# Second experts taken group by group, three token pairs each, with seven-block second products

## The chip, the core and the metric

The kernel runs on one core of a Trainium2 chip, as one launch. TensorE multiplies (PE in the profile) and writes into PSUM; VectorE (DVE), ScalarE (ACT) and GpSimd (POOL) work on what lies in SBUF and, the first two, in PSUM; SyncE (SP) issues nearly all transfers. The metric is the device time of one execution in microseconds; the median of several executions is compared.

## The reference

An attention without softmax, a dense expert with SiLU, and a mixture of four experts with ReLU, whose outputs are weighted with normed probabilities:

```python
def _attn_ref(q, k, v, g_norm) -> np.ndarray:
    kv = np.einsum('bhsd,bhse->bhde', k, v)
    out = np.einsum('bhsd,bhde->bhse', q, kv)
    rms = np.sqrt(np.mean(out * out, axis=-1, keepdims=True) + 1e-06)
    return (out / rms * g_norm).astype(np.float32)
...
    h = x @ w_in
    g = h * (1.0 / (1.0 + np.exp(-h)))
    return (g @ w_out).astype(np.float32)
...
    N, D = x.shape
    E = w1.shape[0]
    p = domain_probs / (domain_probs.sum(-1, keepdims=True) + 1e-09)
    out = np.zeros((N, D), dtype=np.float32)
    for e in range(E):
        h = np.maximum(x @ w1[e], 0.0)
        out += p[:, e:e + 1] * (h @ w2[e])
    return out.astype(np.float32)
```

There are 2304 tokens with 512 features. The dense expert has 2048 hidden features, each of the four others 1024. All is float32.

## The kernel before

**Tiling.** Tokens are cut into three stretches of 768, which the code and this text call pairs, since each holds two halves of 384 columns. Hidden features are cut into groups of 512: four of the dense expert ("first experts", `E1 = 4`), eight of the others ("second experts", `E2 = 8`, two for each expert). A step `n` is one group with one pair. Steps -12 to -1 are the first experts, steps 0 to 23 the second. A step has a first product (features to 512 hidden features) and a second one (hidden back to 512 features, summed into `acc`).

**Precision.** A float32 operand is split into an upper half, which ScalarE writes (`hi`), and a lower half, the rest, which VectorE or GpSimd writes (`lo`). A product of two operands takes three matmuls of halves, 12 matmuls of 128x128 by 128x384 for each of its quarters.

**Seven products.** The operands of a step are two-by-two blocks. By Strassen's scheme in Winograd's form seven products of block sums stand for eight: 84 matmuls for a whole product. A first product is always made so (`first`, blocks into banks `x` and `z` of PSUM). A second product is made so in some steps (`again`: banks `ox`, `oz`; it needs seven hidden operands, c11, c12 taken as t1, t2, t3, t4, c22 and c21, so four differences by `sumh`, and seven additions into `acc` by `gather`), and in the others as four plain blocks of 24 matmuls, 96 in all (`second`: bank `o`; four hidden operands, four gathers). `seven(n)` says which: before, `n >= 8` and five of the first experts' steps.

**Order.** `events` gives each call a time in slots; the calls are sorted by it, and each engine gets its instructions in that order. A slot is one block of 12 matmuls: in a step's window the first products stand at odd slots (`b0 + 1 + 2k`) and the second products of the step before at even ones (`after + 2m`, where `after` is the next step's start). A step with seven second products lasts 14 slots, one with plain ones 15. Each engine runs its queue in order, so an instruction that waits holds up what is queued behind it.

**Loops before.** The second experts run pair by pair: step `n` is pair `n // 8` with group `n % 8`. The features' operands of a pair (`x`, seven tiles of 768 KB, split by `xhi` and `xlo`) stay in SBUF for its eight steps. In the first eight steps the weights are loaded, summed (`sumw`), split (`op1`, `op2`) and put away to DRAM (`put_away`, 14 tiles of 512 KB to a group); steps 8 to 23 get them from there (`get`), eight slots ahead of use. The weight sums of the second products, for which there is no use in plain steps, are made beside steps 0 to 7 too. Pairs 0 and 1 leave after their last step, while the next pair runs: `leave` turns 256 tokens by eight transposes, ScalarE copies them, and ScalarE's queue issues the store. `leave_last` does it for the last pair at the end.

## Time and profile before

| | before |
|---|---|
| median of 3 runs | 1168.19 us (1168.1 to 1168.59) |
| the profiled execution | 1168.03 us, its span 1166.2 us |
| TensorE busy | 1153.6 us, 99% |
| VectorE busy | 866.8 us, 74% |
| ScalarE busy | 499.1 us, 43% |
| GpSimd busy | 315.5 us, 27% |
| granted TensorE clock, mean | 1.0 |
| moved by DMA | 309 MB, 265 GB/s in the mean |

Busy times say which engine is nearly full; the chain that ended last says whose work set the end; a timeline shows where an engine stood still and for whom. Matmuls overlap, so the mean duration of one (335 ns) is not what one costs: that is the distance from start to start. In the windows below, the first number behind a stretch is its length, and then come the busy us of each engine with its count of instructions.

### The profile page before, as it was taken

What the parts mean: (1) busy time and instruction counts of PE and PEld (TensorE: products, weight loads), DVE (VectorE), ACT (ScalarE), POOL (GpSimd) and SP (SyncE); (2) the same over time, 40 slices, a digit from 0 to 9 for tenths busy, and PEclk for the clock granted to TensorE, in tenths of its full rate; (3) what the DMA queues carried; (4) which work ended last, traced back from release to release, by engine and by line L of the source; (5) the groups of instructions that cost most, each with busy time, mean ns of one, the idle gap of its engine ahead of it and who ended that gap; (6) DMA issues with size and microseconds to landing.
All of it is one profiled execution on the core that took longest, in us unless ns stands there. A gap on an engine that the chain in (4) does not pass through costs nothing.

```text
span 1166.2 us, 17617 instructions
## 1 busy us (share of the span) xinstructions
PE 1153.6 (99%) x6769; PEld 1144.8 (98%) x6769; DVE 866.8 (74%) x1010; ACT 499.1 (43%) x720; POOL 315.5 (27%) x196
## 2 busy tenths in 40 slices
PE   9999999999999999999999999999999999999998
PEld 8999999999999999999999999999999999999997
DVE  3997566887887667777777866777888866666776
ACT  4895565455544445434344324333233333233222
POOL 4943311232221324222232312121114221111112
PEclk9999999999999999999999999999999999999999
DMA  9876877566556366987896869898988777878764
GB/s 369 345 270 228 331 256 261 200 212 245 198 189 227 137 203 227 325 296 279 303 324 260 287 222 360 319 330 312 332 312 285 244 258 255 275 258 283 252 199 126
DMA packets 101815, 309.00 MB, mean 265 GB/s; under 512 B 11420, under 2 KB 37988, under 8 KB 101220
## 3 DMA queue, kind: packets, MB, share of 16 engines
q1 hardware_dynamic: 99716, 304.69, 73.6%
q10 hardware_dynamic: 2016, 3.18, 0.7%
q8 instruction: 54, 0.88, 0.3%
q14 instruction: 29, 0.24, 0.1%
...
## 4 chain that ended last, share of the span: by engine, by line
PE 54%; DVE 6%; ACT 2%; issue 2%; DMA 0%; SPq 0%; DVEq 0%; ACTq 0%
PE ps_x L390 15%; PE ps_z L390 11%; PE ps_o L526 10%; PE ps_ox L390 10%; PE ps_oz L390 8%; DVE f L469 1%; ACT hid L164 1%; DVE acc L495 1%; DVE f L433 1%; DVE hid L167 1%; DVE t L477 1%; DVE w L167 1%; PE ps_t L556 0%; DVE s L308 0%; ACT x L164 0%
## 5 line engine op out<-in xcount | busy, mean ns | idle before, releaser
L390 PE MATMUL ps_x<-x,w 128*128 128x384 f32 x1584 | 297.0, 335 | 0.0
L390 PEld LDWEIGHTS ps_x<-x,w 128*128 128x128 f32 x1584 | 277.6, 188 | 0.0
L526 PE MATMUL ps_o<-hid,w 128*128 128x384 f32 x1440 | 268.3, 335 | 1.5 <-ACT hid L164 1.4
L526 PEld LDWEIGHTS ps_o<-hid,w 128*128 128x128 f32 x1440 | 251.2, 188 | 3.4 <-ACT hid L164 2.4
L164 ACT ACTIVATE hid<-f 128x768 fp32r<-128x768 f32 x143 | 120.1, 843 | 243.3 <-DVE f L469 217.5
L390 PE MATMUL ps_z<-x,w 128*128 128x384 f32 x1188 | 222.9, 335 | 0.6 <-DVE f L433 0.6
L390 PEld LDWEIGHTS ps_z<-x,w 128*128 128x128 f32 x1188 | 208.2, 188 | 0.9 <-DVE f L433 0.9
L390 PE MATMUL ps_ox<-hid,w 128*128 128x384 f32 x1008 | 190.2, 336 | 1.2 <-DVE acc L495 1.0
L390 PEld LDWEIGHTS ps_ox<-hid,w 128*128 128x128 f32 x1008 | 176.2, 188 | 2.1 <-ACT hid L164 0.9
L167 DVE TENSOR_TENSOR hid<-f,hid 128x768 fp32r<-128x768 f32 x116 | 124.3, 1072 | 60.6 <-ACT hid L164 59.4
L390 PE MATMUL ps_oz<-hid,w 128*128 128x384 f32 x756 | 142.1, 335 | 1.6 <-DVE acc L495 1.2
L390 PEld LDWEIGHTS ps_oz<-hid,w 128*128 128x128 f32 x756 | 131.9, 188 | 2.7 <-DVE acc L495 2.1
L167 POOL TENSOR_TENSOR hid<-t,hid 128x768 fp32r<-128x768 f32 x32 | 62.7, 1961 | 241.8 <-ACT hid L164 236.0
L167 POOL TENSOR_TENSOR hid<-f,hid 128x768 fp32r<-128x768 f32 x27 | 52.3, 1938 | 210.7 <-ACT hid L164 210.7
L167 POOL TENSOR_TENSOR w<-raw,w 128x512 fp32r<-128x512 f32 x41 | 60.9, 1491 | 178.3 <-ACT w L164 135.2
L164 ACT ACTIVATE hid<-t 128x768 fp32r<-128x768 f32 x64 | 53.9, 843 | 121.0 <-DVE t L477 121.0
L495 DVE TENSOR_TENSOR acc<-ps_ox,acc 128x768 f32<-128x768 f32 x77 | 73.2, 950 | 41.7 <-PE ps_ox L390 41.6
L222 POOL TENSOR_TENSOR full<-full,wd_raw 128x512 int32<-128x512 int32 x32 | 47.7, 1491 | 127.7 <-DVE full L216 93.1
L433 DVE TENSOR_TENSOR f<-ps_z,f 128x768 f32<-128x768 f32 x66 | 62.6, 949 | 20.2 <-PE ps_z L390 20.2
L164 ACT ACTIVATE w<-s 128x512 fp32r<-128x512 f32 x88 | 54.3, 623 | 49.6 <-DVE s L249 18.1
L469 DVE SCALAR_TENSOR_TENSOR f<-f,pb 128x768 f32<-128x768 f32 x72 | 72.5, 1006 | 3.3 <-DMA pb<-p_dram 1.2
L495 DVE TENSOR_TENSOR acc<-ps_oz,acc 128x768 f32<-128x768 f32 x61 | 58.1, 952 | 20.1 <-PE ps_oz L390 19.2
...
## 6 DMA issues: line engine op xcount, KB each, us to landing
...
x<-x_dram SPq DMA_DIRECT2D x63, 768.0 KB, 4.6
raw<-in_w SPq DMA_DIRECT2D x192, 128.0 KB, 3.8
...
x_dram<-x SPq DMA_DIRECT2D x21, 768.0 KB, 6.0
...
```

The costliest lines, as they stand in the source:

```text
L164: self.nc.scalar.activation(t[:, 0], f, AF.Copy)
L167: (eng or self.nc.vector).tensor_tensor(t[:, 1], f, t[:, 0].bitcast(F32), op=ALU.subtract)
L222: self.nc.gpsimd.tensor_tensor(f, f, self.words(c, i, 0, I32), op=ALU.add)
L390: self.nc.tensor.matmul(p[:, f, :HN], w[0][:, a, c : c + 128], x[:, b, kp, :], start=self.FRESH[k] and a == b == kp == 0, stop=b == kp == ...
L433: self.nc.vector.tensor_tensor(t, self.of_ps(n, c), t, op=ALU.add)
L469: self.nc.vector.scalar_tensor_tensor(f, src, 0.0, self.probs(n, int(name[2]) - 1), op0=ALU.max, op1=ALU.mult)
L477: self.nc.vector.tensor_tensor(f, self.f[n, a], self.f[n, b], op=ALU.subtract)
L495: self.nc.vector.tensor_tensor(a, self.of_ps(n, k), a, op=ALU.add)
L526: self.nc.tensor.matmul(self.ps[n, b][:, e, :HN], w[:, u, c : c + 128], h[:, v, kp, :], start=self.count[key] == 1, stop=self.count[key] = ...
```

## The change

The second experts run group by group: step `n` is group `n // 3` with pair `n % 3`, as the first experts did. A group's weights are loaded, summed and split once, in the steps around its first (`weight_events`, with the slots of `W1_AT` and `W2_AT`), and stay in SBUF for three steps. Nothing of them goes to DRAM. The features' operands do: steps 0 to 2 split them (`X_AT`), use them and put them into DRAM, and every later step gets its seven tiles from there (`xget`, 12.4 slots ahead of use). All steps but step 0 have seven second products; step 0 keeps the plain blocks. The differences of hidden parts are written into tiles that are no longer needed, in place of five tiles of their own. The lower halves of t3, t4 and c22 go to GpSimd in all steps from 1 on. All three pairs end in the last three steps, so all six pieces of pairs 0 and 1 leave at the end: one just before the last step's second products, five between them, from SyncE's queue.

```diff
-            self.start[n + 1] = self.start[n] + (self.LONG if n <= E2 else self.SHORT)
+            self.start[n + 1] = self.start[n] + 7 + (7 if self.seven(n - 1) else 8)
...
-        return n >= E2 or n in (-8, -7, -5, -4, -3)
+        return n >= 1 or n in (-8, -7, -5, -4, -3)
...
+    def whi(self, e, i, name):
+        pool, tag = (self.w1_p, "w1") if i == 1 else (self.v_p, "w2b") if name in ("s3", "s4") else (self.w2_p, "w2")
+        t = pool.tile([128, 2, 512], F32R, tag=tag, name=f"w{i}")
+        self.halves[e, i, name] = t, self.raw[e, i, name]
+        self.hi(*self.halves[e, i, name])
+        if i == 1:
+            self.wf[e, self.A.index(name)] = t
+        else:
+            self.w2["f", e, name] = t
...
-    def put_away(self, n, i, k):
-        t = self.w1[n, k] if i == 1 else self.w2[n, self.A[k]]
-        self.nc.sync.dma_start(out=self.w_dram[n * 14 + (i - 1) * 7 + k], in_=t.bitcast(F32).rearrange("p a b -> p (a b)"))
...
+    def slot(self, n, k):
+
+        return 5 - k if k in (2, 3) and (n < 0 or n == 1) else k
...
-        w = self.wf[self.group(n), k] if n < 0 else self.w1.pop((n, k))
-        self.product(self.ps[n, self.INTO[k]], (w, 1), self.x[self.key(n), self.B[k]], k)
-        if n < 0:
+        w = self.wf[self.group(n), k]
+        self.product(self.ps[n, self.INTO[k]], (w, 1), self.x[n, self.B[k]], k)
+        if 0 <= n < NP:
+            self.done_x(n, self.B[k])
+        else:
             del self.x[n, self.B[k]]
-            if self.pair(n) == NP - 1:
-                del self.wf[self.group(n), k]
+        if self.pair(n) == NP - 1:
+            del self.wf[self.group(n), k]
...
-            self.ps[n, b] = self.bank(self.ps2, b, "o")
+            self.ps[n, b] = self.bank(self.ps2, b + (n > -3), "o")
...
-    def leave(self, n, t, b):
-        p = self.bank(self.ps2, n + 1, "t")
+    def leave(self, t, b, pool, i):
+        p = self.bank(pool, i, "t")
         for k in range(2):
             for d in range(KC):
                 c = (b + k) * 128
                 self.nc.tensor.transpose(p[:, k, d * 128 : d * 128 + 128], self.acc[:, t, d, c : c + 128], self.ident)
-        for k in range(2):
-            o = self.o_p.tile([128, DM], F32, tag="o2", name="o2")
-            self.nc.scalar.activation(o, p[:, k, :], AF.Copy)
-            r = t * PW + (b + k) * 128
-            self.nc.scalar.dma_start(out=self.out[r : r + 128, :], in_=o)
+        o = self.x_p.tile([128, 2, DM], F32, tag=f"x{t * 3 + b // 2}", name="o2")
+        self.nc.scalar.activation(o, p, AF.Copy)
+        r = t * PW + b * 128
+        self.nc.sync.dma_start(out=self.out[r : r + 256, :].rearrange("(k p) c -> p k c", p=128), in_=o)
...
+        on_pool = {name: self.nc.gpsimd for name in (("t3", "t4") if n < 0 else ("c22", "t3", "t4"))}
+        late = 0 <= n < self.steps - 1
+        c11, c21, t4 = (5.8, 4.7, 5.6) if late else (4.7, 3.3, 4.6)
+        for at, name in ((b0 + c11, "c11"), (b0 + 10.7, "c22"), (b0 + 12.4, "t1"), (after + 1.11, "t2"), (after + 2.4, "t3"),
+                         (after + c21, "c21"), (after + t4 + 0.9, "t4")):
...
-            lo = at + (0.5 if at < b0 + 12 else 0.005)
-            put(lo, self.hlo, n, name, pool if name in ("t3", "t4") else None, True)
+            lo = at + (0.5 if at < b0 + 12 or late and name == "c21" else 0.005)
+            put(lo, self.hlo, n, name, on_pool.get(name), True)
...
+    X_AT = (
+        ((-12.5, -10.5, -6.7, -8.7, -4.7, -2.7, -0.7), (-11.5, -7.5, -6.5, -1.6)),
+        ((-12.8, -11, -6.8, -8.7, 4.6, 3, 8.2), (-13.8, -7.3, 3.9, 7.3)),
...
+    W1_AT = dict(
+        load=(-23.2, -13), s1=(-11, -7.6), s2=(-10.9, -7.5), s4=(-4.9, -5.1), s3=(-6.9, -4.5),
...
+        b0, i = self.start[(e - E1) * NP], min(e - E1, 1)
+        for at, part in ((self.W1_AT, 1), (self.W2_AT, 2)):
+            load = self.load1 if part == 1 else self.load2
+            for k, (r, c) in enumerate(((1, 0), (1, 1), (0, 0), (0, 1))):
+                put(b0 + at["load"][i] + 0.5 * k, load, e, r, c)
+            for name in ("s1", "s2", "s3", "s4"):
+                put(b0 + at[name][i], self.sumw, e, part, name)
+        ops = dict(zip(self.A, self.W1_AT["op"][i])), self.W2_AT["op"][i]
+        on_pool = (self.A if i == 0 else ("a12", "s3", "a22")), (("a11", "a21", "a22") if i == 0 else ())
+        for part in (1, 2):
+            for name, at in ops[part - 1].items():
+                put(b0 + at, self.whi, e, part, name)
+                put(b0 + at + 0.4, self.flo, e, part, name, pool if name in on_pool[part - 1] else None)
...
+                    put(b0 + at[k], self.xhi, n, name)
+                    put(b0 + at[k] + 0.01, self.xlo, n, name, pool if k in ((0, 1, 5) if n else (1, 3, 5)) else None)
+                    put(b0 + at[k] + 2.5, self.xput, n, name)
+                for k, s in enumerate(sums):
+                    put(b0 + s, self.xsum, t, f"t{k + 1}")
+            else:
+                for k in range(7):
+                    put(self.start[n - 1] + 2 * k + 2.6, self.xget, n, k)
...
-                put(i - lead, self.op1, n, k, pool if k in (1, 4, 6) or n == 0 else None)
-                put(i - lead + 2, self.put_away, n, 1, k)
...
-                for m, k in enumerate(self.ORDER):
-                    put(after + 2 * m, self.again, n, k)
-                    put(after + 2 * m - self.LEAD, self.get, n, 2, k)
...
-            elif q == E2 - 1:
-                for k in range(PW // 256):
-                    put(self.start[n + 3 + k] + 11.5, self.leave, n + 2 + k, t, 2 * k)
...
+                for slot, name in ((5.3 if n else 6.15, "c11"), (10.5, "c22"), (12.5, "c12"), (14.1, "c21")):
+                    put(b0 + slot, self.hhi, n, name)
+                    put(b0 + slot + 0.01, self.hlo, n, name, pool if name == "c22" else None)
+                self.plain_events(put, n)
+        end = self.start[self.steps]
+        for k, at in enumerate((-2.5, 1.3, 2.8, 4.3, 5.8, 7.3)):
+            where = (self.ps2, self.steps + 1) if at < 0 else (self.ps1, k + 1)
+            put(end + at, self.leave, k // 3, k % 3 * 2, *where)
+        for b, (slot, j, i, *ds) in enumerate(((9.5, 1, 0), (11.5, 1, 1), (13, 0, 0), (16, 0, 1, (0,)), (16, 0, 1, (1,)))):
+            put(end + slot, self.leave_last, j, i, b, *ds)
```

On TensorE, the second product of step 1 among the first product of step 2 (`ps_x`, `ps_z`). Before, it is plain blocks into `ps_o`:

```order
L390 MATMUL ps_x<-x_3748,w_4447 128x384 x12
L526 MATMUL ps_o<-hid,w_4431 128x384 x6
L526 MATMUL ps_o<-hid,w_4452 128x384 x6
L390 MATMUL ps_z<-x_3788,w_4485 128x384 x12
L526 MATMUL ps_o<-hid,w_4431 128x384 x6
L526 MATMUL ps_o<-hid,w_4452 128x384 x6
```

After:

```order
L366 MATMUL ps_ox<-hid,w_4115 128x384 x12
L366 MATMUL ps_x<-x_4287,w_3719 128x384 x12
L366 MATMUL ps_oz<-hid,w_4097 128x384 x12
L366 MATMUL ps_z<-x_4323,w_3753 128x384 x12
L366 MATMUL ps_ox<-hid,w_4496 128x384 x12
L366 MATMUL ps_x<-x_4401,w_3794 128x384 x12
```

The two halves of a plain block, each of two weights by six matmuls, have become seven blocks of one weight by twelve, into two banks by turns.

On VectorE, in the middle of a seven-product step. Before, in a step of the last two thirds (`t` are the differences' tiles, `acc` the gathers, `f<-f,pb` the products with the probabilities):

```order
L167 TENSOR_TENSOR hid<-f,hid 128x768
L433 TENSOR_TENSOR f<-ps_z,f 128x768
L469 SCALAR_TENSOR_TENSOR f<-f,pb 128x768
L495 TENSOR_TENSOR acc<-ps_ox,acc 128x2x384
L167 TENSOR_TENSOR hid<-f,hid 128x768
L495 TENSOR_TENSOR acc<-ps_oz,acc 128x2x384
L495 TENSOR_TENSOR acc<-ps_ox,acc 128x2x384
L433 TENSOR_TENSOR f<-ps_x,f 128x768
```

After, the same place in the first step of a group (`s` are weight sums, `raw` loaded weights, `w` split ones):

```order
L149 TENSOR_TENSOR hid<-f,hid 128x768
L149 TENSOR_TENSOR w_5679<-s,w_5679 128x512
L149 TENSOR_TENSOR w_5699<-raw_5518,w_5699 128x512
L464 TENSOR_TENSOR acc<-ps_oz,acc 128x2x384
L289 TENSOR_TENSOR s<-raw_5494,raw_5511 128x512
L289 TENSOR_TENSOR s<-s,raw_5518 128x512
L149 TENSOR_TENSOR w_5727<-s,w_5727 128x512
L149 TENSOR_TENSOR w_5744<-s,w_5744 128x512
L464 TENSOR_TENSOR acc<-ps_ox,acc 128x2x384
L289 TENSOR_TENSOR s<-raw_5535,s 128x512
L289 TENSOR_TENSOR s<-raw_5518,raw_5494 128x512
L411 TENSOR_TENSOR f<-ps_x,f 128x768
```

Between a step's gathers now stand four weight sums and four lower halves of weights.

On TensorE at the end, the transposes `ps_t` of the pieces that leave. Before:

```order
L390 MATMUL ps_ox<-hid,w_10594 128x384 x12
L390 MATMUL ps_oz<-hid,w_10623 128x384 x12
L390 MATMUL ps_ox<-hid,w_10652 128x384 x12
L390 MATMUL ps_oz<-hid,w_10684 128x384 x12
L390 MATMUL ps_ox<-hid,w_10722 128x384 x12
L569 MATMUL ps_t<-ident,acc 128x128 x6
L390 MATMUL ps_oz<-hid,w_10747 128x384 x12
```

After:

```order
L366 MATMUL ps_ox<-hid,w_9619 128x384 x12
L522 MATMUL ps_t<-ident,acc 128x128 x8
L366 MATMUL ps_oz<-hid,w_9647 128x384 x12
L522 MATMUL ps_t<-ident,acc 128x128 x8
L366 MATMUL ps_ox<-hid,w_9664 128x384 x12
L522 MATMUL ps_t<-ident,acc 128x128 x16
L366 MATMUL ps_oz<-hid,w_9788 128x384 x12
L522 MATMUL ps_t<-ident,acc 128x128 x8
L366 MATMUL ps_ox<-hid,w_9855 128x384 x12
L534 MATMUL ps_t<-ident,acc 128x128 x6
```

Five pieces of eight transposes have come between the last second products; the smaller pieces of the last pair (by six) follow as before.

## Rows read from the trace of the kernel before

**Rows 1.** Page, part 1: busy us, share of the span, instructions

```profile
PE 1153.6 (99%) x6769; PEld 1144.8 (98%) x6769; DVE 866.8 (74%) x1010; ACT 499.1 (43%) x720; POOL 315.5 (27%) x196
```

**Rows 2.** Chain that ended last: start us, us, work

```profile
600.57 4.17 PE ps_o L526 x24
```

**Rows 3.** Waits of TensorE: waiter, releaser, us in total, times, longest

```profile
PE ps_o L526 <- ACT hid L164: 1.4, 3, 0.6
PE ps_oz L390 <- DVE acc L495: 1.2, 2, 1.0
```

**Rows 4.** Timeline of TensorE around two stalls: start, us, instruction, [idle before]

```profile
568.13 2.25 PE L526 MATMUL ps_o<-hid,w 128*128 128x384 f32 x12
...
573.28 2.25 PE L390 MATMUL ps_x<-x,w 128*128 128x384 f32 x12
...
917.22 2.25 PE L390 MATMUL ps_oz<-hid,w 128*128 128x384 f32 x12
920.07 2.36 PE L390 MATMUL ps_z<-x,w 128*128 128x384 f32 x12 [0.60 <-DVE f L433]
...
924.99 1.21 PE L390 MATMUL ps_x<-x,w 128*128 128x384 f32 x6
```

**Rows 5.** Groups by form: instruction, count, busy us, mean ns, idle before

```profile
L167 DVE TENSOR_TENSOR hid<-f,hid 128x768 fp32r<-128x768 f32 x116 | 124.3, 1072 | 60.6 <-ACT hid L164 59.4
...
L495 DVE TENSOR_TENSOR acc<-ps_ox,acc 128x768 f32<-128x768 f32 x77 | 73.2, 950 | 41.7 <-PE ps_ox L390 41.6
L469 DVE SCALAR_TENSOR_TENSOR f<-f,pb 128x768 f32<-128x768 f32 x72 | 72.5, 1006 | 3.3 <-DMA pb<-p_dram 1.2
...
L167 POOL TENSOR_TENSOR hid<-f,hid 128x768 fp32r<-128x768 f32 x27 | 52.3, 1938 | 210.7 <-ACT hid L164 210.7
...
L308 DVE TENSOR_TENSOR s<-raw,raw 128x512 f32<-128x512 f32 x32 | 32.0, 1000 | 0.0
...
L477 DVE TENSOR_TENSOR f<-f 128x768 f32<-128x768 f32 x20 | 22.0, 1098 | 1.9 <-ACT f L443 1.8
...
L167 DVE TENSOR_TENSOR w<-raw,w 128x512 fp32r<-128x512 f32 x15 | 12.2, 821 | 11.8 <-ACT w L164 9.4 <-DMA raw<-in_w 2.4
```

**Rows 6.** Timeline of VectorE beside GpSimd in the first experts

```profile
231.58 1.54 POOL L167 TENSOR_TENSOR w<-s,w 128x512 fp32r<-128x512 f32 x1 [13.90 <-ACT w L164]
231.89 2.05 DVE L477 TENSOR_TENSOR f<-f 128x768 f32<-128x768 f32 x1
...
241.23 1.74 POOL L167 TENSOR_TENSOR w<-full,w 128x512 fp32r<-128x512 f32 x1
241.74 0.94 DVE L495 TENSOR_TENSOR acc<-ps_oz,acc 128x768 f32<-128x768 f32 x1
242.61 1.17 DVE L167 TENSOR_TENSOR hid<-f,hid 128x768 fp32r<-128x768 f32 x1
```

**Rows 7.** Busy us of each engine in stretches of 50 us

```profile
250.00:300.00 50.00, 48.61 (x278) 48.00 (x277) 39.65 (x55) 24.62 (x36) 9.92 (x8) 1.00 0.66 236
300.00:350.00 50.00, 50.00 (x290) 50.00 (x289) 44.57 (x49) 24.68 (x35) 14.55 (x8) 1.00 0.55 185
...
1000.00:1050.00 50.00, 50.00 (x293) 49.93 (x292) 32.13 (x35) 15.56 (x20) 10.27 (x6) 1.00 0.78 262
```

**Rows 8.** DMA issues: tensors, queue, count, KB each, median us to landing

```profile
x<-x_dram SPq DMA_DIRECT2D x63, 768.0 KB, 4.6
raw<-in_w SPq DMA_DIRECT2D x192, 128.0 KB, 3.8
```

**Rows 9.** Timeline of TensorE at the end

```profile
1142.75 2.24 PE L390 MATMUL ps_ox<-hid,w 128*128 128x384 f32 x12
...
1156.83 0.82 PE L569 MATMUL ps_t<-ident,acc 128*128 128x128 f32 x6
1157.40 2.37 PE L390 MATMUL ps_ox<-hid,w 128*128 128x384 f32 x12
...
1159.61 1.42 PE L569 MATMUL ps_t<-ident,acc 128*128 128x128 f32 x9
```

318 lines of the change are left out of this document (95 added, 223 removed), and 1 row of the table X_AT.

## The prediction

> **What bounds the kernel now.** The first view is the page's line of busy times [rows 1]: TensorE is busy for 1153.6 us of a span of 1166.2, VectorE for 866.8, ScalarE and GpSimd for less than half. The second is the chain that ended last [rows 2]: through the whole middle it consists of TensorE blocks that follow each other without a hole. There 24 matmuls take 4.17 us, so one costs 0.1738 us, and the planner's slot, a block of 12, costs 2.09 us. The third is the list of TensorE's waits [rows 3]: the two largest that concern matmuls, 1.4 and 1.2 us, are sums over the whole kernel. So the time is the number of matmuls times 0.1738 us, with small stalls, and what the change is worth is the number of matmuls that it takes away, less the stalls that it makes. The reader is to look for stalls made by VectorE, the next engine.
>
> **What it removes on TensorE.** Of the 24 steps of the second experts, the old kernel writes the second product of eight (steps 0 to 7) as four blocks of 24 matmuls, 96 in all; the new one does so in step 0 alone, and takes seven products of 12, or 84, in steps 1 to 23. That is 7 x 12 = 84 matmuls, which the two instruction orders confirm (6591 and 6507 on TensorE). All stand on the path: 84 x 0.1738 = **14.60 us**. The first products, and the transposes that turn the result, keep their number.
>
> **Stalls that go.** Three stalls lie in stretches that are laid out anew. At 570 us a block of the plain second product waits for the upper half of a hidden part from ScalarE: from 568.13 to 573.28 there are 24 matmuls, 5.15 us in place of 4.17, 0.98 late [rows 4]. The same happens, with the same size, at 664.9 us. Both come from the four-block form, whose first block needs two hidden parts at once. At 917 us, in the step in which the features of the third pair are split, 36 matmuls take from 917.22 to 924.99, 7.77 us in place of 6.26, 1.51 late. Together 0.98 + 0.98 + 1.51 = 3.47 us go.
>
> **What comes on VectorE.** Seven steps get seven hidden parts in place of four, so four differences and three more gathers each, and 14 lower halves of weights come over from GpSimd, while GpSimd gets 21 more lower halves of hidden parts. VectorE's sum is 28 differences x 1.10 + 21 gathers x 0.95 + 14 halves x 0.82 [rows 5] = 30.8 + 20.0 + 11.5 = 62 us: (866.8 + 62) / 1152, 81% of the span instead of 74%. This lies beside TensorE as long as no step asks for more than its 168 matmuls last, 29.2 us. In a seven-product step VectorE has 7 gathers and 3 additions at 0.95, 4 products with the probabilities at 1.0, 4 lower halves of hidden parts at 1.07 and 4 differences at 1.10: 22.2 us. The weights come on top, now only once in three steps. The first step of a group adds four sums at 1.0 and four lower halves at 0.82: 29.5 us. These are durations. Where the queue is full the next instruction starts earlier: from 241.74 to 242.61 it is 0.87 us for an instruction of 0.94 [rows 6], a factor of 0.92. So the first step asks for 27.1 us of 29.2, the second (four halves) for 23.5, the third (four sums and three halves of the next group) for 26.4; together 77.0 of 87.6.
>
> Is that too much? In the stretch 300 to 350 us of the old kernel VectorE was busy for 44.57 us of 50, that is 26.0 per 29.2, and TensorE did not wait; in 250 to 300 it was busy for 39.65 and TensorE lost 1.39 [rows 7], which is 0.81 per step. So the bounds for the first step of each of the seven later groups are 0 and 0.81. A gain is excluded, since this step adds work and takes none away. The load of 27.1 is nearest to the row of 300 to 350, and a result has slack: a bank of PSUM that has been filled is written again three slots, 6.3 us, later. I take 0.1 each, **+0.7 us**; with the cover gone it is 5.7.
>
> **The features.** Their split for pairs 1 and 2 moves from steps far apart (7 to 8 and 15 to 16) to steps 0 to 2, one right behind the other, and on VectorE it stands beside seven-product steps. The rows say what such a step loses: 1.51 where the third pair was split, and perhaps nothing where the second was, since the 0.98 there are as large as at 570 us, where nothing was split [rows 4]. So the bounds are 0 and 1.51 for each pair. I take 1.25, twice, near the upper end, as both splits now stand beside seven-product steps, as that of the third pair did: **+2.5 us**.
>
> **Transfers.** 336 transfers of weights, in and out, go; 147 more reads of features come (210 in place of 63) and 21 more writes. SyncE's queue is in order, and its reads wait for TensorE to release the buffer, as the weights' reads did. A read is put 12.4 slots, 26 us, ahead of its use, and lands in 4.6 us [rows 8]. Nothing else on that queue waits for longer than a step: the weights' loads behind it have 4 slots, 8.3 us, for 3.8. The bytes fall, too: 336 times 512 KB go, 168 times 768 KB come. I cost it at nothing; the cover is the 21 us between 26 and 4.6.
>
> **The end.** Six pieces of the result, each eight transposes and a copy, left TensorE in the middle; now one stands just before the last step's second products and five between them. On TensorE their number is the same. In the old end the seven last blocks start at 1142.75 and end at 1159.61, 16.86 us for 84 matmuls (14.60) and two pieces of six transposes (0.57 each, from 1156.83 to 1157.40): 1.12 us is waiting [rows 9]. The transposes now fill that, up to 1.12; against it stand ScalarE's larger copies, after which a bank is free again. I take -0.8, with bounds of -1.12 and +1. The last transfers land as before.
>
> **Sum**, against the profiled execution (1168.03; its span is 1166.2, and 1.8 lies around it): 1168.03 - 14.60 - 3.47 + 0.7 + 2.5 - 0.8 = 1152.4. The median of the runs stands 0.16 higher: **1152.5 us**.
>
> **A rule on ports.** VectorE and GpSimd collide: a GpSimd instruction runs from 231.58 for 1.54 us, a difference on VectorE that starts at 231.89 takes 2.05 us in place of 0.95 and ends after it; a gather, which reads PSUM, takes 0.94 inside another GpSimd instruction (241.23, 1.74 us long) [rows 6]. The Trainium skill, page "SBUF — State Buffer", section "Who interferes with whom", says that a VectorE instruction with two SBUF inputs and a GpSimd instruction that reads SBUF block each other for the whole instruction. The trace agrees in these rows. This speaks against the change, which puts three GpSimd halves into seven more steps. The sum above has the collisions in its means: a difference has a mean of 1.10 against a gather's 0.95, so most instructions miss each other.
>
> **Rivals.** (1) *VectorE is late in each group's first step.* For it: 27.1 us is above the 26.0 that ran without a wait. Against it: such a row lost 0 as well as 0.81. Price: 7 x 0.81 = 5.7 in place of 0.7, 1157.4; with no gain at the end 1158.2. (2) *No new stalls.* For it: the stretch of 300 to 350 us, and the second pair's split, which shows no stall of its own. Against it: the third pair's split cost 1.51. Price: -3.2, 1149.2. (3) *Slower than before: the port makes VectorE the bound.* Were each of a step's three GpSimd halves (1.94 us [rows 5]) to hold up VectorE for its whole length, that would be 5.8 us on top of an average step's 25.7 (77.0 / 3): 31.5 against 29.2, 2.3 us late in each of 23 steps, 1152 + 53 = 1205. It turns the sign when the steps lose over 15.7 / 23 = 0.68 us each, that is from 4.2 us of collisions a step. The skill's rule of the paragraph above gives this if every GpSimd half meets a two-input instruction at its start. Against it: the old steps 8 to 23 have the same three halves, and in 1000 to 1050 us GpSimd is busy for 10.27 and TensorE for 50.00 of 50 [rows 7].
>
> **How the numbers follow.** Forecast 1152.5 (1150.5 to 1155): 0.70. Rival 2: 0.12. Rival 1 (1155 to 1160): 0.14. Rival 3: 0.04. The range runs from rival 2's price to rival 1's without the gain at the end, 1149.2 to 1158.2; about 0.1 is left out. What the measurement can tell from no change is 0.2%, 2.3 us: faster has 0.95, since three cases lie 10 us or more below; within it 0.01; slower 0.04.
>
> **What would show it.** TensorE busy for some 1140 us, with stalls below 1 us apiece and nearly all of them in the feature splits of steps 0 to 2; VectorE's share near 80%, evenly from step 1 on; starts of seven-product steps 29.2 us apart. A gap that returns every three steps is rival 1; a gap in each step, with VectorE at 95%, is rival 3. I am wrong in another way if TensorE waits for a read of features, or if the last transposes wait for ScalarE's copies.

## The result, and the profile after

The changed kernel takes 1148.26 us in the median (1148.04 to 1148.75), the one before 1168.22 in the same runs: a ratio of 0.9829, with a 95% interval of 0.9812 to 0.9846. The forecast was 1152.5, with a range of 1149.2 to 1158.2. The sign and the main term were right; the time came out 4.2 us lower than forecast and 0.94 us below the range. The profiled execution after took 1148.04 us, its span 1146.2 us.

The page's line of busy times after (busy us, share of the span, instructions), to be read against [rows 1]:

```profile
PE 1136.0 (99%) x6685; PEld 1130.1 (99%) x6685; DVE 937.8 (82%) x1073; ACT 514.7 (45%) x728; POOL 329.6 (29%) x196
```

TensorE has 84 instructions fewer, as counted. VectorE has risen by 71 us to 82%, where 62 us and 81% were forecast. The list of TensorE's waits after, without those of the attention at the start and one of 0.3 us at the very end (waiter, releaser, us in total, times, longest):

```profile
PE ps_oz L366 <- DVE acc L464: 1.0, 1, 1.0
PE ps_ox L366 <- DVE acc L464: 0.6, 1, 0.6
...
PE ps_oz L366 <- ACT hid L146: 0.3, 1, 0.3
```

These three lie between 247 and 298 us, in the first experts, and were there before. The waits of [rows 3] for the plain form are gone. In the second experts only one place remains, in the feature splits. TensorE's timeline there (start, us, instruction):

```profile
504.74 2.25 PE L366 MATMUL ps_ox<-hid,w 128*128 128x384 f32 x12
506.82 2.25 PE L366 MATMUL ps_x<-x,w 128*128 128x384 f32 x12
509.11 2.38 PE L366 MATMUL ps_oz<-hid,w 128*128 128x384 f32 x12
511.33 2.25 PE L366 MATMUL ps_z<-x,w 128*128 128x384 f32 x12
```

Twelve matmuls at 0.1738 us make 2.09 us from start to start. From 506.82 to 509.11 it is 2.29 and to the next 2.22, so 0.33 us are lost; with 0.10 at 500.5 us the feature splits lose 0.45 in all. From then until the end of the steps no block starts late. So nothing like [rows 4] is left.

Busy time of each engine in stretches (us; the number of instructions in brackets; then granted clock, DMA share, GB/s), to be read against [rows 7]. The last two are 88 us long, which is a group of three steps (87.6 us):

```profile
250.00:300.00 50.00, 48.75 (x279) 48.14 (x278) 39.75 (x54) 25.07 (x37) 10.26 (x8) 1.00 0.66 238
300.00:350.00 50.00, 50.00 (x289) 50.00 (x288) 44.56 (x50) 24.70 (x35) 14.55 (x8) 1.00 0.54 185
690.00:778.00 88.00, 88.00 (x508) 88.00 (x507) 78.72 (x86) 31.95 (x44) 22.84 (x13) 1.00 0.65 226
1000.00:1088.00 88.00, 88.00 (x508) 88.00 (x507) 78.72 (x86) 31.95 (x44) 22.78 (x12) 1.00 0.66 228
```

In 88 us VectorE is busy for 78.7 us, and over one group (504 matmuls, 87.64 us) for 78.4; the forecast had 77.0. TensorE is busy throughout. The groups of VectorE's instructions after (count, busy us, mean ns, idle before), against [rows 5]; the products with the probabilities, priced at 1.0 us, take 1.2:

```profile
L149 DVE TENSOR_TENSOR hid<-f,hid 128x768 fp32r<-128x768 f32 x148 | 150.6, 1019 | 54.6 <-ACT hid L146 54.4
...
L464 DVE TENSOR_TENSOR acc<-ps_ox,acc 128x768 f32<-128x768 f32 x105 | 99.7, 949 | 14.3 <-PE ps_ox L366 13.3
L446 DVE SCALAR_TENSOR_TENSOR f<-f,pb 128x768 f32<-128x768 f32 x72 | 86.6, 1203 | 2.5
...
L149 DVE TENSOR_TENSOR w<-s,w 128x512 fp32r<-128x512 f32 x74 | 52.3, 712 | 6.3 <-ACT w L146 5.7
```

The reads of features, against [rows 8], and the end, against [rows 9] (first fence: DMA issues with count, KB each, median us to landing; second: TensorE's timeline):

```profile
x<-x_dram SPq DMA_DIRECT2D x210, 768.0 KB, 4.3
```

```profile
1127.48 1.91 PE L522 MATMUL ps_t<-ident,acc 128*128 128x128 f32 x16
1129.14 2.34 PE L366 MATMUL ps_oz<-hid,w 128*128 128x384 f32 x12
1131.32 1.03 PE L522 MATMUL ps_t<-ident,acc 128*128 128x128 f32 x8
1132.11 2.33 PE L366 MATMUL ps_ox<-hid,w 128*128 128x384 f32 x12
```

No read of features is waited for. At the end the pieces stand between the products without an idle time.

**Where the 20.0 us went.** Set against the pitch of 0.1738 us, matmul by matmul, the two profiled executions differ by: 84 matmuls fewer, -14.60; the three stalls that the forecast named, -3.47; a stall of 1.11 at 413 to 422 us that went too, which the forecast had overlooked; +0.45 in the feature splits; and -1.26 at the end and in the middle, where the pieces of the result used to leave. Together -19.99.

### The profile page after: what moved, and what is told of

It is laid out like the page before. It is cut to its first block, busy times and chain, and to the rows that moved or that the text cites. A ratio compares the mean times of both kernels' runs of the same rounds, so it can differ in the third digit from the quotient of the medians.

```text
span 1146.2 us, 17111 instructions
## 1 busy us (share of the span) xinstructions
PE 1136.0 (99%) x6685; PEld 1130.1 (99%) x6685; DVE 937.8 (82%) x1073; ACT 514.7 (45%) x728; POOL 329.6 (29%) x196
## 4 chain that ended last, share of the span: by engine, by line
PE 90%; DVE 4%; DMA 3%; ACT 2%; issue 0%; POOL 0%; ACTq 0%; POOLq 0%; DVEq 0%
PE ps_x L366 22%; PE ps_ox L366 19%; PE ps_z L366 17%; PE ps_oz L366 15%; PE ps_o L495 10%; PE ps_h L394 4%; DMA kv_raw<-in_kv 2%; DVE hid L149 1%; PE p_o L855 1%; ACT hid L146 1%; DMA wd_raw<-in_wd 1%; PE ps_kv L833 1%; DVE acc L464 1%; DVE w L149 1%; PE p_t L882 0%; DVE f L451 0%
## 5 line engine op out<-in xcount | busy, mean ns | idle before, releaser
L146 ACT ACTIVATE hid<-f 128x768 fp32r<-128x768 f32 x228 | 189.9, 843 | 369.3 <-DVE f L451 194.4
L149 POOL TENSOR_TENSOR hid<-f,hid 128x768 fp32r<-128x768 f32 x80 | 157.9, 1974 | 549.2 <-ACT hid L146 425.4
L366 PE MATMUL ps_ox<-hid,w 128*128 128x384 f32 x1344 | 252.4, 335 | 0.6 <-DVE acc L464 0.6
L366 PEld LDWEIGHTS ps_ox<-hid,w 128*128 128x128 f32 x1344 | 234.7, 188 | 1.1 <-ACT hid L146 0.9
L149 DVE TENSOR_TENSOR hid<-f,hid 128x768 fp32r<-128x768 f32 x148 | 150.6, 1019 | 54.6 <-ACT hid L146 54.4
L366 PE MATMUL ps_oz<-hid,w 128*128 128x384 f32 x1008 | 189.6, 335 | 1.3 <-DVE acc L464 1.0
L495 PE MATMUL ps_o<-hid,w 128*128 128x384 f32 x768 | 142.0, 335 | 0.0
L495 PEld LDWEIGHTS ps_o<-hid,w 128*128 128x128 f32 x768 | 134.1, 188 | 0.0
L451 DVE TENSOR_TENSOR f<-f 128x768 f32<-128x768 f32 x112 | 111.0, 991 | 3.2 <-ACT f L421 1.8
L446 DVE SCALAR_TENSOR_TENSOR f<-f,pb 128x768 f32<-128x768 f32 x72 | 86.6, 1203 | 2.5
L406 ACT ACTIVATE f<-ps_x 128x768 f32<-128x768 f32 x66 | 53.3, 808 | 36.9 <-PE ps_x L366 36.8
L149 DVE TENSOR_TENSOR w<-s,w 128x512 fp32r<-128x512 f32 x74 | 52.3, 712 | 6.3 <-ACT w L146 5.7
```

What stands on the lines that cost most here:

```text
L146: self.nc.scalar.activation(t[:, 0], f, AF.Copy)
L149: (eng or self.nc.vector).tensor_tensor(t[:, 1], f, t[:, 0].bitcast(F32), op=ALU.subtract)
L366: self.nc.tensor.matmul(p[:, f, :HN], w[0][:, a, c : c + 128], x[:, b, kp, :], start=self.FRESH[k] and a == b == kp == 0, stop=b == kp == ...
L406: self.nc.scalar.activation(t, self.of_ps(n, c), AF.Copy)
L446: self.nc.vector.scalar_tensor_tensor(f, src, 0.0, self.probs(n, int(name[2]) - 1), op0=ALU.max, op1=ALU.mult)
L451: self.nc.vector.tensor_tensor(f, self.f[n, a], self.f[n, b], op=ALU.subtract)
```

## Experiments

The forecast's two prices for VectorE (2.5 us in the feature splits, 0.7 in the groups' first steps) came out as 0.45 and 0. So the question is what keeps VectorE in time, and how near it is to being late. All runs stand beside runs of the kernel before, of 1168.1 to 1169.5 us. Where no interval is given a time is that of one run; the stalls are read from the traces, as excess over the pitch.

### Slots of the feature splits, and places of the tiles

```diff
-        ((-12.8, -11, -6.8, -8.7, 4.6, 3, 8.2), (-13.8, -7.3, 3.9, 7.3)),
+        ((-11.8, -10, -5.8, -7.7, 4.6, 3, 8.2), (-12.8, -6.3, 3.9, 7.3)),
```

(for pairs 1 and 2)

> The changed kernel, with one part undone: the splits and sums of the features of the token pairs 1 and 2 stand at the old slots again (first splits 1 slot later, two sums 1 slot later), all else as changed. Theory S (the new slots of these splits made the old stall of 1.51 us at the third pair's split vanish): TensorE loses about 1.5 us more in each of the two split steps, so its excess over the pitch in 455 to 550 us rises from 0.45 to some 3 us, and the time from 1148.3 to 1150 to 1151.5 us. Rival G (the stall went with the later hidden parts, or with the lower half that GpSimd took over): no change, excess 0.3 to 0.8 us, time 1147.9 to 1148.8.

1148.76 us. Between 450 and 550 us TensorE lost 0.40, as with the new slots. Theory S falls. The other 0.7 us are lost at 297 us, ahead of all that the edit moves; that wait took between 0.4 and 1.1 us beyond the pitch in the kernels of this section.

```diff
-        return 5 - k if k in (2, 3) and (n < 0 or n == 1) else k
+        return 5 - k if k in (2, 3) and (n < 0 or n in (0, 2)) else k
```

> The changed kernel, with the places of the feature tiles 2 and 3 exchanged again in steps 0 and 2 and not in step 1, as they stood for step 0 before. Theory: the 1.11 us that TensorE lost at 413 to 422 us before came from here, because the split of step 0's third feature operand needs a tile that the step before still reads: ScalarE waits there some 2.7 us for TensorE, VectorE gets 1.5 us late, and TensorE loses 1.0 to 1.2 us near 413 to 422 us; time 1149.2 to 1149.6. Rival (the stall went because the weights' preparation beside it became lighter, or because the banks of the second product were shifted by one): nothing is lost there, time 1148.0 to 1148.6.

1150.0 us, above the theory's 1149.2 to 1149.6. The span is 1.6 us longer than after (1147.8 against 1146.2); 1.12 of that are lost at 414 to 423 us, where the changed kernel loses nothing. First ScalarE's timeline in this run, then TensorE's:

```profile
398.85 0.85 ACT L146 ACTIVATE x<-acc 128x768 fp32r<-128x768 f32 x1 [2.69 <-PE ps_z L366]
```

```profile
411.17 3.63 PE L495 MATMUL ps_o<-hid,w 128*128 128x384 f32 x20
415.40 0.96 PE L495 MATMUL ps_o<-hid,w 128*128 128x384 f32 x4 [0.59 <-ACT hid L146]
```

ScalarE stands for 2.69 us at the head of its queue, because the tile that it wants to write is still read by TensorE (in the kernel before 2.70, at 398.16 us). What is queued behind it reaches the hidden part late, 13 us further on. In the changed kernel, where this tile has another place, the same 24 matmuls run through:

```profile
410.72 4.33 PE L495 MATMUL ps_o<-hid,w 128*128 128x384 f32 x24
```

So the overlooked 1.11 us is one line of the change, `slot`, shown by undoing it.

### Which part of the new step keeps VectorE in time

```diff
-        on_pool = {name: self.nc.gpsimd for name in (("t3", "t4") if n < 0 else ("c22", "t3", "t4"))}
+        on_pool = {name: self.nc.gpsimd for name in ("t3", "t4")}
```

> The changed kernel, with the lower half of the hidden part c22 of the second experts on VectorE instead of GpSimd in all steps. Theory M (VectorE still has room, since an instruction in a full queue takes less than its duration): VectorE's busy time rises by 22 to 24 us, GpSimd's falls by some 45, TensorE loses nothing in the middle, time 1147.5 to 1149.5. Rival F (the first step of a group is full, as its row of 89% in 690 to 778 us suggests): TensorE loses 0.5 to 0.9 us in each of the seven later groups, time 1152 to 1155, with gaps every three steps. If the stalls of the third pair's split in the kernel before came from this instruction, 1.5 us come back near 500 us.

1148.38 us, no stall beyond those of the changed kernel. VectorE's busy time rose by 11.7 us, not 22: the 23 instructions added bring 22, and the collisions with GpSimd, which now does 23 less, fall by 10, nearly all of it on the products with the probabilities (77.8 us in place of 86.6). Theory M holds; the reason given for its size was incomplete.

```diff
-        late = 0 <= n < self.steps - 1
+        late = False
```

> The changed kernel, with the upper halves of the hidden parts c11, c21 and t4 and the last difference of the second experts at the slots that the first experts use (4.7, 3.3 and 4.6 in place of 5.8, 4.7 and 5.6). Theory L (the later slots keep VectorE's additions, which release TensorE's banks, ahead of this work): TensorE loses 0.5 to 1.5 us at the feature splits and some tenths in each group's first step, time 1149 to 1154. Rival N (VectorE has room at these places too): time 1147.9 to 1148.8.

**1183.81 us**: 35.6 slower than the changed kernel, and 14 slower than the kernel before. The slots are those of the first experts; the kernel before had still others in its seven-product steps of the second experts (c21 at 3.3, t4's difference at 1.2 and its halves at 5.5). Both expectations were far too small. TensorE's waits:

```profile
PE ps_ox L366 <- DVE w L149: 14.6, 7, 2.6
PE ps_oz L366 <- DVE acc L464: 11.5, 8, 1.8
```

Seven waits for a weight's half and eight for a gather: about one of each per group. VectorE has the same 1073 instructions as in the changed kernel, but they take 32.7 us longer (page of this run; then groups of VectorE):

```profile
PE 1145.2 (97%) x6685; PEld 1134.4 (96%) x6685; DVE 970.5 (82%) x1073; ACT 509.6 (43%) x728; POOL 329.6 (28%) x196
```

```profile
L149 DVE TENSOR_TENSOR hid<-f,hid 128x768 fp32r<-128x768 f32 x148 | 174.7, 1181 | 72.0 <-ACT hid L146 71.7
...
L149 DVE TENSOR_TENSOR w<-s,w 128x512 fp32r<-128x512 f32 x74 | 73.5, 1000 | 10.3 <-ACT w L146 10.3
```

Against 1019 and 712 ns after, these are the instructions that read two operands from SBUF. Two of them in the timeline of this run, with the GpSimd instruction that each meets, and what TensorE makes of it:

```profile
641.51 1.85 POOL L149 TENSOR_TENSOR hid<-f,hid 128x768 fp32r<-128x768 f32 x1 [10.49 <-issue]
648.26 2.05 POOL L149 TENSOR_TENSOR hid<-f,hid 128x768 fp32r<-128x768 f32 x1 [4.89 <-ACT hid L146]
```

```profile
642.15 2.03 DVE L149 TENSOR_TENSOR hid<-f,hid 128x768 fp32r<-128x768 f32 x1 [0.78 <-ACT hid L146]
...
648.56 2.30 DVE L149 TENSOR_TENSOR w<-s,w 128x512 fp32r<-128x512 f32 x1
```

```profile
650.91 1.32 PE L366 MATMUL ps_ox<-hid,w 128*128 128x384 f32 x6 [2.24 <-DVE w L149]
```

Each ends only after GpSimd's has ended, as in [rows 6]. The late weight half is what TensorE waits for at 650.91. But VectorE also waits for ScalarE's upper halves for 17 us longer (71.7 against 54.4), so collisions and order were still to be told apart, and which of the slots it was.

### Which slots, and whether it is the collisions

```diff
-        c11, c21, t4 = (5.8, 4.7, 5.6) if late else (4.7, 3.3, 4.6)
+        c11, c21, t4 = (4.7, 4.7, 5.6) if late else (4.7, 3.3, 4.6)
```

> The changed kernel, with the upper half of the hidden part c11 alone at its old slot (4.7 in place of 5.8). With all three groups of slots undone the time was 1183.8 us: TensorE lost 41.9 us against its pitch instead of 6.4, in a pattern that returns every three steps, and VectorE's instructions took 33 us longer, nearly all of it as instructions that overlap a GpSimd half. Theory P (what the late slots do is keep VectorE's instructions with two SBUF inputs clear of GpSimd's halves; c11's upper half moves none of these against GpSimd): excess 6 to 8 us, 1148 to 1150. Rival Q (the late slots keep the additions that free TensorE's banks ahead of the halves, c11's first of all): a third or more of the 35 us, over 1158.

1147.74 us, and in five more runs of the same kernel 1148.04 (below). c11's late slot is of no use; without it the 0.45 us in the feature splits go. Rival Q falls as far as c11 goes.

```diff
-        c11, c21, t4 = (5.8, 4.7, 5.6) if late else (4.7, 3.3, 4.6)
+        c11, c21, t4 = (5.8, 3.3, 5.6) if late else (4.7, 3.3, 4.6)
...
-            lo = at + (0.5 if at < b0 + 12 or late and name == "c21" else 0.005)
+            lo = at + (0.5 if at < b0 + 12 else 0.005)
```

> The changed kernel, with the upper and lower half of the hidden part c21 alone at the old slot (3.3 in place of 4.7). Theory P: the collisions go with the lower half of c21, which at 3.3 stands in VectorE's queue where GpSimd's half of t3 begins: VectorE's busy time rises by 20 us or more, TensorE's excess by 15 to 35, 1163 to 1183. Rival Q (order ahead of the additions matters, c11's above all): 1148 to 1152.

1149.55 us. VectorE's busy time rose by 13.1 us to 950.9, but TensorE lost only 1.4 us more. The time lies in rival Q's range, and theory P's numbers, 20 us or more and 15 to 35, were too high: collisions come, and there is room for them. So neither c11 nor c21 alone carries the 35 us.

```diff
-        c11, c21, t4 = (5.8, 4.7, 5.6) if late else (4.7, 3.3, 4.6)
+        c11, c21, t4 = (5.8, 3.3, 4.6) if late else (4.7, 3.3, 4.6)
```

(with the line for `lo` as above)

> The changed kernel, with the halves of c21 and the last difference t4 at their old slots (3.3 and 4.6) and c11 alone late. Theory P: as with all undone, 1178 to 1184, VectorE busy for some 970 us. Rival Q (c11 carries it): 1148 to 1155.

1170.67 us, between the two expectations: the room is gone. VectorE is busy for 962.5 us, 24.7 more than in the changed kernel, and TensorE loses 22 us more.

```diff
-        late = 0 <= n < self.steps - 1
+        late = False
...
-        self.lo(self.h[n, name.replace("c", "b")], self.f[n, name], eng)
+        h = self.h[n, name.replace("c", "b")]
+        if n > 0 and eng is not None:
+            self.nc.scalar.activation(h[:, 1], self.f[n, name], AF.Copy)
+        else:
+            self.lo(h, self.f[n, name], eng)
```

> All late slots undone, as in the run of 1183.8 us, but GpSimd's three lower halves of each second-expert step from step 1 on are not computed: ScalarE writes a copy into their place (the differences of t3, t4 and c22 are left out). VectorE's queue stays as it was. Theory P (collisions with GpSimd make VectorE late): VectorE's busy time falls by some 60 us to below 915, TensorE's excess after 430 us from 36 to below 5 us, 1147 to 1152. Rival Q (the order in VectorE's queue, with waits for ScalarE's upper halves at its head, makes it late): over 1165.

1147.78 us: with the slots of the run of 1183.8 us, but without GpSimd's halves, all 36 us are back. Its page:

```profile
PE 1135.5 (99%) x6685; PEld 1130.3 (99%) x6685; DVE 894.4 (78%) x1073; ACT 562.2 (49%) x797; POOL 190.0 (17%) x127
```

The same 1073 instructions of VectorE, in the same order as there, take 76.1 us less. Theory P holds: without the collisions the order alone costs nothing. Nor was it that TensorE stood for GpSimd's halves themselves: none of its waits in the run of 1183.8 us was for GpSimd. And VectorE's waits for ScalarE's upper halves are even longer here than there:

```profile
L149 DVE TENSOR_TENSOR hid<-f,hid 128x768 fp32r<-128x768 f32 x148 | 151.4, 1024 | 87.1 <-ACT hid L146 86.8
```

The Trainium skill, page "SBUF — State Buffer", section "Who interferes with whom", says that a VectorE instruction with two SBUF inputs contends with a GpSimd instruction that reads SBUF, and that one with at most one SBUF input, outside its two-port modes, does not. The traces agree: the gathers, which read one operand from PSUM, keep a mean of 947 to 954 ns after and in the runs above and below, while groups with two operands in SBUF go up, to 1181 above and 1521 below.

### How much room there is

In the next kernels a lower half is written a second time, right behind the first.

```diff
             put(lo, self.hlo, n, name, on_pool.get(name), True)
+            if n > 0 and name in ("c11", "c21"):
+                put(lo + 0.001, self.hlo, n, name, None, True)
```

> The changed kernel, with the lower halves of the hidden parts c11 and c21 written twice on VectorE in steps 1 to 23: 46 instructions of 0.95 us more, some 0.87 us each in a full queue, so 40 to 44 us of VectorE and none of GpSimd. In a group of three steps (87.6 us) VectorE is busy for 78.7 us now. Theory M (VectorE has 9 us or more of room in a group; pure load of 5.2 to 5.7 us fits): TensorE loses less than 2 us, time 1148 to 1150. Rival F (no room in the first step of a group): 0.5 to 2 us in each of seven groups, 1152 to 1162.

1189.72 us. Rival F was right in kind, but its price was too low: 41 us for 46 instructions, with waits for gathers in nearly every step (27 waits, 32.5 us).

```diff
             put(lo, self.hlo, n, name, on_pool.get(name), True)
+            if n > 0 and name not in on_pool:
+                put(lo + 0.001, self.hlo, n, name, None, True)
```

> The same with the four lower halves that VectorE writes per step (c11, t1, t2, c21) written twice: 92 instructions more, 80 to 87 us, or 10.4 to 11.4 us in a group of three steps. Theory M, by summed durations: 78.7 + 11.4 = 90 of 87.6 us, over by 2.5 us a group and more in the first step, so 15 to 30 us lost, 1163 to 1180. Rival O (instructions in a full queue overlap, so the room is nearer 16 us than 9 a group): under 8 us lost, 1148 to 1156.

1232.57 us. Both expectations fell.

```diff
             put(lo, self.hlo, n, name, on_pool.get(name), True)
+            if n > 0 and name in on_pool:
+                put(lo + 0.001, self.hlo, n, name, on_pool[name], True)
```

> The changed kernel, with GpSimd's three lower halves of each step from 1 to 23 written twice: 69 instructions of 1.9 us more on GpSimd, which is idle for 70% of the span, and no more on VectorE. Theory P (each GpSimd half that meets a two-input instruction of VectorE makes that one about 1 us longer): VectorE's busy time rises by 30 to 70 us without an instruction more, TensorE's excess by 10 to 40 us, 1158 to 1188. Rival N (they meet seldom or there is room): VectorE up by less than 20 us, time under 1152.

1208.77 us, worse than theory P's range, as is VectorE's rise. This run adds no work to VectorE at all. Its page, and two groups of VectorE:

```profile
PE 1156.2 (96%) x6685; PEld 1140.2 (94%) x6685; DVE 1021.2 (85%) x1073; ACT 513.6 (43%) x728; POOL 485.7 (40%) x265
```

```profile
L446 DVE SCALAR_TENSOR_TENSOR f<-f,pb 128x768 f32<-128x768 f32 x72 | 109.5, 1521 | 2.5
L464 DVE TENSOR_TENSOR acc<-ps_ox,acc 128x768 f32<-128x768 f32 x105 | 99.6, 949 | 9.8 <-PE ps_ox L366 9.7
```

69 instructions on an engine that is idle for 70% of the span cost 60 us: 83.4 us more of VectorE's time, through collisions alone. TensorE's largest waits here are for gathers (35.0 us in 20 waits), none for GpSimd.

The next three ask whether own work and collisions use one room, or whether the place ahead of a gather decides. The first two have the edit of the lower halves from the kernel without GpSimd's halves, with the late slots as changed.

```diff
             put(lo, self.hlo, n, name, on_pool.get(name), True)
+            if n > 0 and name in ("c11", "c21"):
+                put(lo + 0.001, self.hlo, n, name, None, True)
```

> The changed kernel with its late slots, GpSimd's three lower halves of each step from 1 to 23 not computed (ScalarE writes a copy into their place), and the lower halves of c11 and c21 written twice on VectorE. With GpSimd at work the second part alone gave 1189.7 us, and brought 27 us of collisions beside its own 40 us. Theory R (load and collisions eat from one room in VectorE's queue, and the kernel as changed has nearly used it up by collisions): without them the 40 us fit, TensorE loses less than 1 us after 430 us, 1147.3 to 1149. Rival L (an instruction more at this place, ahead of a gather that frees a bank, makes TensorE wait by itself): 1165 to 1190.

```diff
             put(lo, self.hlo, n, name, on_pool.get(name), True)
+            if n > 0 and name not in on_pool:
+                put(lo + 0.001, self.hlo, n, name, None, True)
```

> The same with the lower halves of c11, t1, t2 and c21 written twice, 80 us more on VectorE, without GpSimd's halves. Theory R: 80 us are more than the 56 us that the collisions took before, so part of it shows: 5 to 35 us lost, 1153 to 1183. If there is more room than the collisions took: under 1150. Rival L: 1190 to 1235, as with GpSimd at work.

And with GpSimd at work:

```diff
             put(lo, self.hlo, n, name, on_pool.get(name), True)
+            if n > 0 and name in ("t1", "t2"):
+                put(lo + 0.001, self.hlo, n, name, None, True)
```

> The changed kernel, GpSimd at work, with the lower halves of t1 and t2 written twice instead of those of c11 and c21: the same 46 instructions and 40 us, at another place in the step. Theory R (the sum in a step decides): as with c11 and c21, 1175 to 1195. Rival L (the place decides): under 1160.

1148.24, 1169.73 and 1185.85 us. The instructions that cost 41 us beside GpSimd's halves cost nothing without them, and at another place in the step they cost nearly as much (38). So theory R's three forecasts came true and rival L falls; that it isn't quite one room shows in the table below. Without GpSimd's halves the 46 instructions bring 51.8 us, not 40, so fewer than 27 us were collisions. The stretch of one group in the changed kernel (above: VectorE 78.72 of 88, TensorE 88.00), then in the runs with c21 and c21 with t4 early, then in the first two of these:

```profile
690.00:778.00 88.00, 88.00 (x508) 88.00 (x507) 80.30 (x86) 31.72 (x45) 22.70 (x13) 1.00 0.68 226
```

```profile
690.00:778.00 88.00, 85.72 (x491) 84.92 (x491) 80.51 (x84) 29.66 (x42) 20.85 (x12) 1.00 0.65 220
```

```profile
690.00:778.00 88.00, 88.00 (x508) 88.00 (x507) 79.73 (x93) 38.20 (x53) 4.34 (x3) 1.00 0.67 226
```

```profile
690.00:778.00 88.00, 85.74 (x492) 85.10 (x491) 82.86 (x96) 37.98 (x53) 3.09 (x3) 1.00 0.65 218
```

Where TensorE waits, 88 us hold less than a group, so these rows can't be set side by side as they stand. Counted over whole groups (504 matmuls each, from 690 us on), VectorE is busy for 78.4 us in the changed kernel, 79.4 in the first of these and 80.1 to 80.6 with c21 early, and a group lasts 87.64 us in all of them. With c21 and t4 early it is busy for 82.2 us or more and a group lasts at least 90.6; in the second of these it is 85.3 and 90.4. So the room ends between 80.6 and 82.2 us in these runs, and the changed kernel is some 2 to 4 us below that. The rest of a longer group is time in which VectorE's queue stands.

Set against the run without GpSimd's halves (894.4 us of VectorE, 23 steps), the page totals give one table:

| run | VectorE above 894.4 us | of it per step | slower than the changed kernel |
|---|---|---|---|
| changed kernel | 43.4 | 1.9 | 0 |
| 46 halves twice, no GpSimd halves | 51.8 | 2.3 | 0.0 |
| c22 on VectorE | 55.1 | 2.4 | 0.1 |
| c21 early | 56.5 | 2.5 | 1.3 |
| c21 and t4 early | 68.1 | 3.0 | 22.4 |
| all early | 76.1 | 3.3 | 35.6 |
| 92 halves twice, no GpSimd halves | 97.5 | 4.2 | 21.5 |
| t1, t2 twice | 111.1 | 4.8 | 37.6 |
| c11, c21 twice | 111.9 | 4.9 | 41.5 |
| GpSimd's halves twice | 126.8 | 5.5 | 60.5 |
| 92 halves twice | 165.9 | 7.2 | 84.3 |

Up to 2.5 us per step nothing or little shows; the next half microsecond per step, 11.6 us in all, costs 21 us. It isn't a single curve: own work alone (97.5 us) costs no more than 68.1 us of collisions. Why collisions weigh more than as many microseconds of own work isn't settled; that they come in lumps at the same place in each step, ahead of a gather, is a guess.

### Further steps by seven blocks, and late slots elsewhere

```diff
-        return n >= 1 or n in (-8, -7, -5, -4, -3)
+        return n >= -5 or n in (-8, -7)
...
-            dict(s1=6.6, s4=10.4, s3=11.5, a11=7.2, a12=8.6, a21=15.2, a22=17.7, s2=29.4),
+            dict(a11=6.5, s1=8, s2=8.6, s4=15.5, s3=19.2, a12=20.4, a22=21.5),
```

(and the banks' turns and the last first-expert group's splits that follow from it)

> The changed kernel, with the second products by seven blocks in the steps -2, -1 and 0 as well, the last ones in plain form behind the first group: 3 x 12 = 36 matmuls x 0.1738 = 6.26 us fewer. VectorE gets 7 instructions more in each and is busy for 65 to 77% there now. Theory M: 1141.5 to 1142.5 with no new stall. Rival F (the hidden parts of these steps, which are placed as in the first experts, meet the features' splits and make VectorE late): 1 to 3 us come back, 1143 to 1146.

1163.08 us, a ratio to the kernel before of 0.9957 (0.9943 to 0.9971): 14.8 slower than the changed kernel. 36 matmuls are gone, 6.26 us, and TensorE loses 21.9 us more, nearly all between 396 and 525 us. VectorE's and TensorE's timeline at the largest wait of the first of these steps:

```profile
403.37 2.56 DVE L323 TENSOR_TENSOR acc<-acc 128x768 f32<-128x768 f32 x1 [1.74 <-POOL x L149]
405.86 0.94 DVE L464 TENSOR_TENSOR acc<-ps_oz,acc 128x768 f32<-128x768 f32 x1
```

```profile
406.85 2.35 PE L366 MATMUL ps_oz<-hid,w 128*128 128x384 f32 x12 [2.59 <-DVE acc L464]
```

VectorE's queue stands 1.74 us for a feature half on GpSimd, then collides for 1.6, and the gather behind it is late. Neither expectation held: the shares of busy time, 65 to 77%, had looked like room.

```diff
-        return n >= 1 or n in (-8, -7, -5, -4, -3)
+        return n >= 0 or n in (-8, -7, -5, -4, -3)
...
-        c11, c21, t4 = (5.8, 4.7, 5.6) if late else (4.7, 3.3, 4.6)
+        c11, c21, t4 = (4.7, 4.7, 5.6) if late else (4.7, 3.3, 4.6)
```

(and the first group's second weights nearly at the later groups' slots, the banks' turns, and the second weights' lower halves a11, a21 and a22 on GpSimd in all groups, in the changed kernel in the first alone, which the expectation does not name)

> The changed kernel with the second product of step 0 by seven blocks too (12 matmuls x 0.1738 = 2.09 us fewer), with the upper half of c11 at its old slot (0.5 us fewer in the run of that alone), and the first group's second weights at the slots of the later groups. The steps -2 and -1 keep the plain form, since with them VectorE was late by 22 us. Theory R: step 0 adds 7 us of VectorE where 41 of 62 us are used, and some collisions with the features' halves on GpSimd: between 1145.5 without a new stall and 1149 with 3 us of them. If it is above 1150, the features' split of step 1 leaves no room beside a seven-block product.

1150.45 us, 0.9847 (0.983 to 0.9863): 2.2 slower than the changed kernel in the median, with intervals that overlap. 2.09 us of matmuls went, and 4.74 came in one place, beside the second pair's feature split, as the last sentence above had it. Of these, two waits for gathers make 3.1 us, and a block at a lower granted clock the rest. The later groups, with more work on GpSimd, lose nothing. TensorE's timeline and the busy times of two short stretches there:

```profile
465.69 2.35 PE L366 MATMUL ps_oz<-hid,w 128*128 128x384 f32 x12 [0.74 <-DVE acc L464]
467.88 2.25 PE L366 MATMUL ps_z<-x,w 128*128 128x384 f32 x12
472.03 3.92 PE L366 MATMUL ps_ox<-hid,w 128*128 128x384 f32 x12 [1.91 <-DVE acc L464]
```

```profile
455.00:472.00 17.00, 14.39 (x82) 13.75 (x80) 16.00 (x15) 8.19 (x12) 8.17 (x4) 1.00 0.68 258
472.00:475.70 3.70, 3.67 (x12) 3.67 (x13) 3.63 (x5) 0.84 (x1) 0.91 (x1) 0.54 1.00 315
```

```diff
-        late = 0 <= n < self.steps - 1
-        c11, c21, t4 = (5.8, 4.7, 5.6) if late else (4.7, 3.3, 4.6)
+        late = n < self.steps - 1
+        c11, c21, t4 = (4.7, 4.7, 5.6) if late else (4.7, 3.3, 4.6)
```

> The changed kernel, with the late slots of c21 and t4 for the seven-block steps of the first experts too (steps -8, -7, -5, -4, -3), and c11 early everywhere. Theory R: where the late slots keep VectorE clear of GpSimd's halves they can take away part of the 2.75 us that TensorE loses between 200 and 300 us, two waits there being for gathers behind instructions that overlap GpSimd: 0.5 to 2.5 us fewer, and 0.5 for c11, 1145.3 to 1147.3. If the collisions there only move to other instructions: 1147.5 to 1150.

1149.45 us, 0.9838 (0.9825 to 0.9852). In the first experts the 0.99 us between 200 and 250 us fell to 0.18, and the 1.76 between 250 and 300 rose to 4.16, by one wait of 2.4 us for a gather and ten matmuls of 320 ns behind it. The gather stands behind a weight's half that takes 2.32 us beside a hidden half on GpSimd (at 251.56): the collisions moved on, as the second expectation had it. By the times it can't be told from the changed kernel. A slot that is right in one kind of step is not right in another.

> The changed kernel, with c11 alone at its old slot, timed in more rounds: between 1147.4 and 1148.3, since 0.45 us of waits for ScalarE near 500 us go and nothing else moves.

1148.04 us (1147.97 to 1148.24), a ratio of 0.9826 (0.9813 to 0.984). The 0.45 us are gone from its trace; by the times it can't be told from the changed kernel. No version that is measurably better than the changed kernel was found.

## Why the prediction was wrong where it was, point by point

- **The bound, and the matmuls taken away**: right. The time is the number of matmuls times their pitch. 84 went, and -14.60 us is what the traces show.
- **Stalls that go**: right, -3.47, all three. Incomplete: a fourth of 1.11 us, at 413 to 422 us, was not named. It hung on the place of a feature tile, a line that the diff showed; undoing that line brings the stall back.
- **The features, +2.5**: this is the step that failed most; it measured 0.45. The price came from what a split had lost in a step of the kernel before. That stall begins where c21's lower half, at slot 3.3, meets the feature half that GpSimd writes behind a hidden half (VectorE, then GpSimd, before):

```profile
915.91 2.37 DVE L167 TENSOR_TENSOR hid<-f,hid 128x768 fp32r<-128x768 f32 x1 [1.42 <-ACT hid L164]
```

```profile
915.60 1.87 POOL L167 TENSOR_TENSOR x<-acc,x 128x768 fp32r<-128x768 f32 x1
```

The change puts c21 at 4.7 and moves t4 too, which stood in the diff and in no term of the sum. With c21 back at 3.3 the two meet again (2.35 us, at 484.79) and the stretch of 450 to 550 us loses 1.4; with all the first experts' slots it loses 3.1; with these slots and without GpSimd's three halves of a step, nothing. So the later slots, and not the new slots of the splits, keep it at 0.45. What the old step would have lost there, and so whether 2.5 was right for it, isn't shown: no run has all of its slots.

- **The groups' first steps, +0.7**: measured 0. The load was sized well (77.0 of 87.6 forecast, 78.4 measured), but placing it between rows of 0 and 0.81 was not safe. The row's 1.39 us is idle time of TensorE; against the pitch that stretch lost 1.9. And with the first experts' slots each group loses 4.7 us ((41.9 - 6.4 - 2.7) / 7, that is the excess of that run less the changed kernel's and less what the feature splits lost), and some 12 us more of collisions in all 23 steps (56.5 to 68.1 in the table) are what lies between almost no loss and 22 us. That is the sign of rival 1, at nearly six times its price. The forecast of nearly nothing was right with the late slots only.
- **The end, -0.8**: measured -1.26, together with the places in the middle from which the pieces went away, which the forecast had taken as equal.
- **Transfers, at nothing**: right; the reads land in 4.3 us.
- **The sum of the misses**: 2.05 + 0.70 + 1.11 + 0.46 = 4.32 us between the profiled executions, all to one side. Hence the time below the low end: that was rival 2's price, which held no new stall at all but counted neither the overlooked one nor the end's further 0.46.
- **Rival 2** (no new stalls) is what happened. Against it stood the row of the third pair's split, which did not hold with the new slots.
- **Rival 3** (the port makes VectorE the bound) was given 0.04 and is one table of slots away: with c21 and t4 early the kernel is about as slow as before (1170.67 against 1168.54), with c11 too it is slower (1183.81). Its turning point was put at 4.2 us of collisions a step; the runs put it at 3.0 beyond those of the kernel without GpSimd's halves. The argument against it, that the old steps had the same three halves and TensorE never waited, overlooked that VectorE was busy there for 32.13 us of 50 [rows 7] and now for 44.94 (the same stretch after), and that the slots were others.
- **What would show it**: TensorE at 1136 for 1140, VectorE at 82% for 80%, stalls below 1 us and, in the second experts, only in the splits: as written.
